# Retention of the later chunks in 64x64 matmuls, four abreast, with the decay in a table of masks

## The chip, the cores and the metric

The kernel runs on one core of one Trainium2 chip. The metric is the device time of one execution in microseconds. Five engines matter: TensorE (PE in the profile; PEld are its weight loads), VectorE (DVE), ScalarE (ACT), GpSimd (POOL) and the queue that issues the DMAs (SP). Each engine works through its own instructions in the order in which they were written, and waits on semaphores for the others. Matmuls write to PSUM, which has eight banks of 512 fp32 columns for each of 128 partitions.

## What is computed

Four sequences of 576 tokens with eight heads of 64 go through a causal linear attention with a decay for each head (retention), and the result through two feed-forward layers. Cut to its core:

```python
scores = q @ k.T / sqrt(64)                     # per batch and head, 576 x 576
gamma  = 1 - 2.0 ** (-5 - arange(8))            # one decay for each head
ret    = scores * where(rel >= 0, gamma ** rel, 0)   # rel = query - key
x      = (ret @ v), heads side by side          # 2304 tokens x 512
x      = relu(x @ w1_in) ** 2 @ w1_out          # 512 -> 2048 -> 512
h      = x @ w2_in
out    = (h * clip(h + 3, 0, 6) / 6) @ w2_out
```

All arrays are fp32.

## The kernel before

**Phases and blocks.** Phase 0 is retention and the first layer, phase 1 the second layer. The 2304 tokens are cut into five blocks of 512 or 384 for either phase (`BLOCKS`). A block takes 16 steps `f`, one for each 128 of the 2048 hidden features. In a step the main loop (from line 443) writes, in this order: `h_part` of the step after (12 matmuls of line 288 into `h`, then ACT's and DVE's work that makes `g` of `h`: lines 298 to 308), one piece of retention, and `a_part` of this step (12 matmuls of lines 329 or 331, which add to the accumulators `acc`). The operands of these matmuls are split into a high and a low part of type fp32r, so there are three products of each. So on PE a step is 12 matmuls `h`, the piece of retention, and 12 matmuls `acc`, and `acc` of a step waits for the `g` that ACT and DVE make.

**Weights.** In block 0 the weights of the first layer come in and are unpacked, step by step: ACT scales them (lines 110, 111), DVE joins the halves (126, 127) and casts every second tile (136), ACT casts the others (138), and POOL makes the low part (140, `w`). This is written between the pieces above, so all of it stands in the same queues.

**Retention.** The tokens are also cut into 18 chunks of 128. Chunks 0 to 3 are done before the first block; the chunks of block b+1 are done during block b, one chunk in four steps: slot 0 `prep_chunk` (POOL multiplies q by gamma^(t+1)/8, line 187, and v by gamma^-(t+1), line 189), slot 1 `scores`, slot 2 `values`, slot 3 `states` and the loads of the chunk two ahead. A chunk's pieces:

- `scores` (line 204): for each of eight heads k^T q, 64 rows of weights by 128 columns, fp32. Two heads lie in the two halves of the rows, in two banks `sc0` and `sc1`. DVE multiplies each bank by a mask of ones and zeros into `p` (line 208).
- `values` (line 221): for each head v^T p, 128 rows by 64 columns, two heads in the two halves of the columns, into one bank `o`; then, where a sequence doesn't begin with the chunk, four full matmuls of the running state with q (line 231). ACT and DVE split `o` into the two parts of `x` (239, 242).
- `states` (line 254): for each head k^T v, into `st`; DVE adds the old state (268) or only scales (266), and multiplies by gamma^128 (269; POOL does that from chunk 4 on).

A sequence has 4.5 chunks: chunks 0 and 9 begin one (`fresh`), 4 and 13 hold the end of one and the beginning of the next (`straddle`), 8 and 17 end one (`ends`, no state is made).

**PSUM.** Four banks hold `acc` (and the scores of chunks 0 to 3), two hold `h` (tag "h"), two hold everything else of retention (tag "at": `sc`, `o`, `st` in turns). The last of the first four chunks makes `o` in two halves (`parts=2`).

An fp32 matmul is two passes in the built program, each a weight load and a matmul of its own, and so two records in the trace; an fp32r matmul is one.

Of the kernel before, what the change touches and what calls it, by code (L numbers as in the profile page):

```python
# [32 lines left out]

VD0 = 0
GC0 = VD0 + H
MK0 = GC0 + NPAIR
QD0 = MK0 + 2 * P
NCONST = QD0 + NPAIR * P


def constants():

    gamma = 1.0 - 2.0 ** (-5.0 - np.arange(H, dtype=np.float64))
    t = np.arange(P, dtype=np.float64)
    c = np.zeros((P, NCONST), np.float64)
    for p in range(NPAIR):  # L50
        for e in range(2):
            g = gamma[2 * p + e]
            c[64 * e : 64 * e + 64, QD0 + p * P : QD0 + (p + 1) * P] = g ** (t + 1) / np.sqrt(D)
            c[64 * e : 64 * e + 64, GC0 + p] = g**P
    c[:, VD0 : VD0 + H] = gamma[None, :] ** -(t[:, None] + 1)
    causal = t[:, None] <= t[None, :]
    half = (t[:, None] < 64) == (t[None, :] < 64)
    c[:, MK0 : MK0 + P] = causal
    c[:, MK0 + P : MK0 + 2 * P] = causal & half
    return c.astype(np.float32)  # L60
# [3 lines left out]
def retention_moe_kernel(ctx: ExitStack, tc, qk, kv, w1, w2, cst, out):  # L64
# [82 lines left out]
    gc = con[:, GC0 : GC0 + NPAIR]  # L147
    state = [apool.tile([P, NPAIR, P], F32, tag=f"s{i}", name=f"state{i}") for i in range(2)]
# [6 lines left out]
    def load_chunk(c):  # L155
# [10 lines left out]
        if c == 0:  # L166
            nc.sync.dma_start(con[:, QD0:], cst[:, QD0:])
# [17 lines left out]
    def prep_chunk(c, eng):  # L185
# [5 lines left out]
    probs = {}  # L191

    def scores(c, pool=None, tag="at"):
        _, straddle, _ = where(c)
        m0 = MK0 + (P if straddle else 0)
        mask = con[:, m0 : m0 + P].unsqueeze(1).to_broadcast([P, NPAIR, P])
        q, kt, _, _ = ch[c]
        sc = [
            (pool or ps_at).tile([P, NPAIR, P], F32, tag=tag, name=f"sc{e}_{c}") for e in range(2)
        ]  # L200
        for p in range(NPAIR):
            for e in range(2):
                r = slice(64 * e, 64 * e + 64)
                nc.tensor.matmul(sc[e][:, p, :], kt[r, p, :], q[r, p, :], start=True, stop=True)  # L204
        for e in range(2):
            pool, tag = (wpool, f"w{NF - 4}_{e}") if c < n0 and c % 2 else (apool, f"p{e}")
            t = pool.tile([P, NPAIR, P], F32, tag=tag, name=f"p{e}_{c}")
            nc.vector.tensor_tensor(t, sc[e], mask, ALU.mult)  # L208
            probs[c, e] = t

    def values(c, xt, off, parts=1, then=None):
        q, _, _, v = ch[c]
        fresh, straddle, _ = where(c)
        np_ = NPAIR // parts
        for i in range(parts):
            ps = slice(i * np_, (i + 1) * np_)
            o = ps_at.tile([P, np_, P], F32, tag="at", name=f"o_{c}_{i}")
            for p in range(i * np_, (i + 1) * np_):
                for e in range(2):
                    h = 2 * p + e  # L220
                    nc.tensor.matmul(  # L221
                        o[64 * e : 64 * e + 64, p % np_, :],
                        v[:, h * D : (h + 1) * D],
                        probs[c, e][:, p, :],
                        start=p % np_ == 0,
                        stop=fresh and p % np_ == np_ - 1,
                    )
            if not fresh:
                n = 64 if straddle else P
                for p in range(i * np_, (i + 1) * np_):  # L230
                    nc.tensor.matmul(  # L231
                        o[:, p % np_, 0:n],
                        state[c % 2][:, p, :],
                        q[:, p, 0:n],
                        start=False,
                        stop=p % np_ == np_ - 1,
                    )
            hi = xt[:, 0, ps, off : off + P]
            nc.scalar.activation(hi, o, AF.Copy)
            if then is not None:  # L240
                then()
            nc.vector.tensor_tensor(xt[:, 1, ps, off : off + P], o, hi.bitcast(F32), ALU.subtract)  # L242

    def states(c):
        _, _, k, v = ch[c]
        fresh, straddle, ends = where(c)
        if ends:
            return
        k0 = 64 if straddle else 0
        st = ps_at.tile([P, NPAIR, 64], F32, tag="at", name=f"st_{c}")  # L250
        for p in range(NPAIR):
            for e in range(2):
# [3 lines left out]
                    k[k0:P, h * D : (h + 1) * D],  # L256
                    v[k0:P, h * D : (h + 1) * D],
# [3 lines left out]
        for e in range(2):  # L261
# [3 lines left out]
            if fresh or straddle:  # L265
                nc.vector.tensor_tensor(s, st[r], g, ALU.mult)
            else:
                nc.vector.tensor_tensor(s, st[r], s0, ALU.add)  # L268
                (nc.vector if c < n0 else nc.gpsimd).tensor_tensor(s, s, g, ALU.mult)  # L269
# [41 lines left out]
    def a_part(ph, blk, f):  # L311
# [4 lines left out]
        if f == 0:  # L316
            accs[ph, blk] = [
                ps_acc.tile([P, 512], F32, tag="acc", name=f"acc_{ph}_{blk}_{d}")
                for d in range(n_acc)
            ]  # L320
# [208 lines left out]
```

## Time and profile before

| | us |
|---|---|
| median of 3 runs | 886.58 (886.45 to 886.61) |
| the profiled execution | 886.73 |
| its span (first to last instruction) | 885.0 |
| PE busy in the span | 871.4 |
| DVE busy | 457.9 |
| ACT busy | 226.9 |
| POOL busy | 96.8 |
| clock granted to TensorE, mean | 0.999 |

The span is cut into engines' busy times, idle times and what ended these. Matmuls are pipelined, so two that follow each other overlap in the rows: what a matmul costs is read from the distance between starts, not from its duration. A row of the timeline has start, duration, engine, line, operation, output and inputs, shape and count, and in brackets the idle time of the engine just before with what ended it. Retention lies in the stretch from 5 to 396 us; block 0 ends on PE at 131 us, and the first layer's last block has no retention beside it.

### The profile page before, as it was taken

How to read it: one execution, taken by the hardware profiler on the slowest of the kernel's cores; microseconds unless marked ns; L12 is line 12 of the kernel's file. 1: busy time of each engine (PE TensorE's matmuls, PEld its weight loads, DVE VectorE, ACT ScalarE, POOL GpSimd, SP SyncE). 2: the span in 40 equal slices, each digit the busy share in tenths (PEclk: the TensorE clock that was granted, in tenths of full speed). 3: DMA queues.
4: the chain of work that ended last, by engine and by line, in shares of the span. 5: the costliest groups of instructions: out<-in, count | busy, mean ns of one | idle time of the engine just before them, and what ended most of it. 6: DMA issues, size and time to landing. Idle time of an engine off the chain costs nothing.

```text
span 885.0 us, 11676 instructions
## 1 busy us (share of the span) xinstructions
PE 871.4 (98%) x4752; PEld 748.3 (85%) x4752; DVE 457.9 (52%) x796; ACT 226.9 (26%) x392; POOL 96.8 (11%) x89
## 2 busy tenths in 40 slices
PE   8899999999999999999999999999999999999998
PEld 7677789999888899998888898888888888888997
DVE  6888874534434344334779776334343433343332
ACT  2556551111111111113556551111111111111111
POOL 3445550301012001110000000000000000000000
PEclk9999999999999999999999999999999999999999
DMA  9844501212110111105566300200020001000000
GB/s 335 349 156 147 198 25 72 73 48 69 44 44 24 48 48 49 48 1 170 192 214 209 131 13 1 71 1 13 1 83 1 13 13 63 0 10 35 14 1 36
DMA packets 26261, 67.73 MB, mean 77 GB/s; under 512 B 2912, under 2 KB 5088, under 8 KB 26208
## 3 DMA queue, kind: packets, MB, share of 16 engines
q1 hardware_dynamic: 26208, 67.00, 21.6%
q8 instruction: 37, 0.61, 0.3%
q14 instruction: 16, 0.13, 0.0%
HBM read 57.55 MB, written 9.44 MB: 76 GB/s over the span
## 4 chain that ended last, share of the span: by engine, by line
PE 90%; DVE 5%; issue 3%; DMA 1%; ACT 1%; SPq 0%; POOL 0%; DVEq 0%; POOLq 0%
PE h L288 41%; PE acc L331 22%; PE acc L329 20%; PE o L221 2%; PE o L231 2%; PE sc L204 1%; DVE wt L127 1%; DVE wt L126 1%; PE st L254 1%; DVE r L299 1%; ACT g L305 1%; DMA raw<-w_dram 1%; DVE p L208 1%; DMA q<-qk_dram 1%; DVE state L269 0%
## 5 line engine op out<-in xcount | busy, mean ns | idle before, releaser
L288 PE MATMUL h<-x,w 128*128 128x512 f32 (+2 forms) x1932 | 421.6, 367 | 0.0
L288 PEld LDWEIGHTS h<-x,w 128*128 128x128 f32 x1932 | 352.1, 188 | 47.6 <-POOL w L140 0.2
L329 PE MATMUL acc<-g,w 128*128 128x512 f32 (+1 forms) x960 | 215.2, 372 | 0.3 <-ACT g L305 0.3
L331 PE MATMUL acc<-w,g 128*128 128x512 f32 x864 | 210.1, 391 | 0.0
L329 PEld LDWEIGHTS acc<-g,w 128*128 128x128 f32 x960 | 172.6, 188 | 25.0 <-ACT g L305 0.7
L331 PEld LDWEIGHTS acc<-w,g 128*128 128x128 f32 x864 | 161.6, 188 | 32.6 <-DVE g L308 0.2
L302 DVE SCALAR_TENSOR_TENSOR r<-r,h 128x512 f32<-128x512 f32 (+1 forms) x80 | 50.7, 634 | 204.8 <-ACT r L301 204.6
L299 DVE TENSOR_TENSOR r<-r,h 128x512 f32<-128x512 f32 (+1 forms) x80 | 50.6, 632 | 159.9 <-ACT r L298 159.8
L301 ACT ACTIVATE r<-h,con 128x512 f32<-128x512 f32 (+1 forms) x80 | 51.7, 646 | 310.3 <-PE h L288 304.7
L308 DVE TENSOR_TENSOR g<-r,g 128x512 fp32r<-128x512 f32 (+1 forms) x160 | 105.9, 662 | 16.2 <-ACT g L305 11.2
L298 ACT ACTIVATE r<-h 128x512 f32<-128x512 f32 (+1 forms) x80 | 44.1, 552 | 245.6 <-PE h L288 238.4
L307 DVE CAST g<-r 128x512 fp32r<-128x512 f32 (+1 forms) x144 | 58.6, 407 | 14.3
L140 POOL TENSOR_TENSOR w<-wt,w 128x512 fp32r<-128x512 f32 x32 | 44.1, 1377 | 55.7 <-ACT w L138 36.1
L127 DVE CUSTOM_DVE_ANT_0 wt<-raw,wt 128x1024 uint16<-128x1024 uint16 x64 | 47.5, 742 | 3.9
L110 ACT ACTIVATE raw<-raw 128x512 f32<-128x512 f32 x64 | 42.5, 664 | 1.0 <-DMA raw<-w_dram 1.0
L111 ACT ACTIVATE raw<-raw 128x512 int32<-128x512 uint32 x64 | 42.5, 664 | 0.0
L138 ACT ACTIVATE w<-wt 128x512 fp32r<-128x512 f32 x48 | 29.6, 626 | 18.9 <-DVE wt L127 18.9
L269 POOL TENSOR_TENSOR state<-state,con 64x256 f32<-64x256 f32 x18 | 11.1, 617 | 206.9 <-DVE state L268 206.2
L126 DVE TENSOR_SCALAR wt<-raw 128x512 int32<-128x512 int32 x64 | 30.1, 470 | 0.5 <-issue 0.3
L221 PE MATMUL o<-p,kv 128*64 128x128 f32 x288 | 21.1, 279 | 4.7 <-DVE x L242 2.3
L187 POOL TENSOR_TENSOR q<-q,con 128x512 f32<-128x512 f32 x17 | 22.8, 1341 | 22.4 <-DMA q<-qk_dram 21.8
L221 PEld LDWEIGHTS o<-p,kv 128*64 128x64 f32 x288 | 15.9, 136 | 10.2 <-DVE p L208 3.9
(32 smaller groups left out, 288.0 us busy)
## 6 DMA issues: line engine op xcount, KB each, us to landing
raw<-w_dram SPq DMA_DIRECT2D x64, 512.0 KB, 5.6
q<-qk_dram SPq DMA_DIRECT2D x36, 256.0 KB, 3.1
kv<-kv_dram SPq DMA_DIRECT2D x14, 512.0 KB, 3.4
out_dram<-ev SPq DMA_DIRECT2D x18, 256.0 KB, 2.0
x<-ev SPq DMA_DIRECT2D x12, 256.0 KB, 2.3
x1r<-x SPq DMA_DIRECT2D x12, 256.0 KB, 4.3
kv<-kv_dram SPq DMA_DIRECT2D x8, 256.0 KB, 6.2
x<-ev SPq DMA_DIRECT2D x8, 192.0 KB, 1.9
```

Source lines behind the costliest of these rows:

```text
L127: nc.vector.tensor_tensor(ti, ti, low, ALU.add)
L140: eng.tensor_tensor(w[:, 1, :], t, w[:, 0, :].bitcast(F32), ALU.subtract)
L221: nc.tensor.matmul(o[64 * e : 64 * e + 64, p % np_, :], v[:, h * D : (h + 1) * D], probs[c, e][:, p, :], start=p % np_ == 0, stop=fresh an ...
L288: nc.tensor.matmul(hp[:, ts], w[:, wi, c * P : (c + 1) * P], x[:, xi, c, ts], start=k == 0, stop=k == 3 * NC - 1,)
L298: nc.scalar.activation(r, hp[:, :nb], AF.Relu)
L299: nc.vector.tensor_tensor(r, r, hp[:, :nb], ALU.mult)
L301: nc.scalar.activation(r, hp[:, :nb], AF.Relu, bias=con3)
L302: nc.vector.scalar_tensor_tensor(r, r, 6.0, hp[:, :nb], ALU.min, ALU.mult)
L307: nc.vector.tensor_copy(g[:, 0, :nb], r)
L308: nc.vector.tensor_tensor(g[:, 1, :nb], r, g[:, 0, :nb].bitcast(F32), ALU.subtract)
L329: nc.tensor.matmul(acc[d][:, :nb], wt[:, sl], gt, start=first, stop=stop)
L331: nc.tensor.matmul(acc[d], gt[:, sl], wt, start=first, stop=stop)
```

## The change

- **Chunks 4 to 17, shape.** Every product of scores, values and states is cut into 64x64 tiles of weights. Two halves of the keys of two heads stand on the four quarters of the PE array: the row half says which group of heads (0 to 3 or 4 to 7), the column half which head of a pair. The scores of keys 0 to 63 meet 128 queries, those of keys 64 to 127 only the 64 that come after; where a chunk straddles two sequences both halves meet 64.
- **PSUM.** Retention has one tile of two banks, one bank for each row half. `sc` takes 384 columns of each, the states the other 128; later the same tile is `o`. The accumulators are two tiles of two banks.
- **Decay.** The mask is now a table with gamma^rel/8 in it (`con` from `DK0` on, 776 columns, loaded by a DMA of its own behind the first weights), so q and k of the scores are used as they come. DVE multiplies 768 columns in one operation (two of 256 where the chunk straddles).
- **States** come directly behind the scores in the same slot, of k scaled by gamma^(127-t) (`scale_k`, POOL, slot 0); POOL multiplies the old state by gamma^128 beforehand (`age_state`, slot 0) and DVE adds. q for the state product is scaled behind the scores (`scale_q`, POOL, slot 1). Slot 3 only loads.
- **Block 0** begins its three chunks two steps later (f = 2 in place of 0).
- **Loads** of k and v come in two DMAs of 64 partitions, so that a row half holds its group of heads.
- **Chunks 0 to 3** keep their products; the scores of a chunk are one tile of two banks with one multiplication of 1024 columns, `o` lies in the banks of `h`, and the fourth chunk isn't cut in halves any more.

Cut to its core:

```diff
-    ps_acc = ctx.enter_context(tc.tile_pool(name="ps_acc", bufs=4, space=bass.MemoryType.PSUM))
+    ps_acc = ctx.enter_context(tc.tile_pool(name="ps_acc", bufs=2, space=bass.MemoryType.PSUM))
     ps_h = ctx.enter_context(tc.tile_pool(name="ps_h", bufs=2, space=bass.MemoryType.PSUM))
-    ps_at = ctx.enter_context(tc.tile_pool(name="ps_at", bufs=2, space=bass.MemoryType.PSUM))
+    ps_at = ctx.enter_context(tc.tile_pool(name="ps_at", bufs=1, space=bass.MemoryType.PSUM))
...
-            nc.sync.dma_start(kv_t, kv[c])
+            for g in range(2):
+                nc.sync.dma_start(
+                    kv_t[64 * g : 64 * g + 64].rearrange("t x (r e) -> t x r e", r=2),
+                    kv[c, :, :, 4 * D * g : 4 * D * (g + 1)].rearrange("(r t) x e -> t x r e", r=2),
+                )
...
+    def first_scores(c):
+        sc = ps_acc.tile([P, 2, NPAIR, P], F32, tag="acc", name=f"sc_{c}")
...
+        nc.vector.tensor_tensor(
+            t.rearrange("p e n t -> p (e n) t"), sc.rearrange("p e n t -> p (e n) t"), mask, ALU.mult
+        )
...
+    def first_values(c, xt, then=None):
+        o = ps_h.tile([P, NPAIR, P], F32, tag="h", name=f"o_{c}")
...
+    def scale_q(c):
+        if where(c)[0]:
+            return
+        nc.gpsimd.tensor_tensor(q, q, qd3, ALU.mult)
+
+    def scale_k(c):
+        if where(c)[2]:
+            return
+        nc.gpsimd.tensor_tensor(k3, k3, kd.unsqueeze(2).to_broadcast([P, H, D]), ALU.mult)
...
+    def scores(c):
+        at = ps_at.tile([P, 2, 512], F32, tag="at", name=f"sc_{c}")
+        sc = at[:, :, : 2 * MKW].rearrange("p e (j t) -> p e j t", j=2)
+        for j in range(2):
+            for i, keys in enumerate(halves(2)):
+                ts = span(c, i)
+                for g, rg in enumerate(halves(2)):
+                    for e, re in enumerate(halves(2)):
+                        nc.tensor.matmul(
+                            sc[rg, e, j, P * i : P * i + ts.stop - ts.start],
+                            kt[re, 2 * g + j, keys],
+                            q[re, 2 * g + j, ts], start=True, stop=True)
+        if not ends:
+            st = at[:, :, 2 * MKW :].rearrange("p g (j d) -> p g j d", j=2)
+            for j in range(2):
+                for i in range(first, 2):
+                    for g, rg in enumerate(halves(2)):
+                        for e, re in enumerate(halves(2)):
+                            h = 4 * i + 2 * j + e
+                            nc.tensor.matmul(st[re, g, j, :],
+                                k[rg, h * D : (h + 1) * D], v[rg, h * D : (h + 1) * D],
...
+            nc.vector.tensor_tensor(
+                t.rearrange("p e j t -> p e (j t)"), at[:, :, : 2 * MKW],
+                decay.rearrange("p e j t -> p e (j t)"), ALU.mult)
+        for e, re in enumerate(halves(2)):
+            s = diagonal(c + 1, e)
+            if fresh or straddle:
+                nc.vector.tensor_copy(s, st[re])
+            else:
+                nc.vector.tensor_tensor(s, st[re], s, ALU.add)
...
+    def age_state(c):
+        for e, re in enumerate(halves(2)):
+            nc.gpsimd.tensor_tensor(diagonal(c + 1, e), diagonal(c, e), g, ALU.mult)
...
-                j, slot = f // 4, f % 4
+                j, slot = divmod(f - 2 if blk == 0 else f, 4)
...
                     if slot == 0:
-                        prep_chunk(c, nc.gpsimd)
+                        scale_k(c)
+                        age_state(c)
                     elif slot == 1:
                         scores(c)
+                        scale_q(c)
                     elif slot == 2:
                         values(c, xs[0, blk + 1], j * P)
                     else:
-                        states(c)
                         load_chunk(c + 2)
```

PE in block 1, steps 2 to 4, beside chunk 7, before. `sc0`, `sc1` are the two banks of scores, which alternate for eight rows; `h_0_1_2` is the `h` of phase 0, block 1, step 2, and `acc_0_1_0` the first of four accumulators.

```order
L288 MATMUL h_0_1_2_1379<-x_0_1_442,w_0_2_0_410 128x384 x12
L204 MATMUL sc0_7_1398<-q_7_897 128x128
L204 MATMUL sc1_7_1399<-q_7_897 128x128
...
L288 MATMUL h_0_1_4_1470<-x_0_1_442,w_0_4_0_538 128x384 x12
L254 MATMUL st_7_1489<-kv_7_898 64x64 x8
L329 MATMUL acc_0_1_0_1363<-g_0_1_3_1440,w_0_3_1_541 128x384 x2
```

The same place in the changed kernel:

```order
L427 MATMUL h_0_1_2_1420<-x_0_1_430,w_0_2_0_398 128x384 x12
L316 MATMUL sc_7_1439<-q_7_1019 64x128 x4
L316 MATMUL sc_7_1439<-q_7_1019 64x64 x4
L316 MATMUL sc_7_1439<-q_7_1019 64x128 x4
L316 MATMUL sc_7_1439<-q_7_1019 64x64 x4
L331 MATMUL sc_7_1439<-kv_7_1020 64x64 x16
...
L427 MATMUL h_0_1_4_1543<-x_0_1_430,w_0_4_0_508 128x384 x12
```

Eight matmuls of scores became 16 smaller ones, and the states, 16 matmuls in place of eight, moved up two steps into the same visit; behind `h_0_1_4` no retention stands any more.

POOL in block 0 before: `w` is a tile of weights in work (phase, step, half). `q_4` and `kv_4` belong to chunk 4, which stands among the tiles of steps 1 to 3.

```order
L140 TENSOR_TENSOR w_0_1_1_416<-wt_0_1_1_413,w_0_1_1_416 128x512
L187 TENSOR_TENSOR q_4_221<-q_4_221,con_92 128x512
L189 TENSOR_TENSOR kv_4_222<-kv_4_222,con_92 128x512
L140 TENSOR_TENSOR w_0_3_0_473<-wt_0_3_0_447,w_0_3_0_473 128x512
L140 TENSOR_TENSOR w_0_2_1_476<-wt_0_2_1_470,w_0_2_1_476 128x512
```

POOL in the changed kernel, the same stretch and a little further:

```order
L158 TENSOR_TENSOR w_0_1_1_404<-wt_0_1_1_401,w_0_1_1_404 128x512
L158 TENSOR_TENSOR w_0_3_0_457<-wt_0_3_0_433,w_0_3_0_457 128x512
L158 TENSOR_TENSOR w_0_2_1_460<-wt_0_2_1_454,w_0_2_1_460 128x512
L158 TENSOR_TENSOR w_0_4_0_508<-wt_0_4_0_486,w_0_4_0_508 128x512
L158 TENSOR_TENSOR w_0_3_1_511<-wt_0_3_1_505,w_0_3_1_511 128x512
L293 TENSOR_TENSOR kv_4_217<-kv_4_217,con_92 128x512
L158 TENSOR_TENSOR w_0_5_0_560<-wt_0_5_0_538,w_0_5_0_560 128x512
L158 TENSOR_TENSOR w_0_4_1_563<-wt_0_4_1_557,w_0_4_1_563 128x512
L287 TENSOR_TENSOR q_4_216<-q_4_216,con_92 128x512
```

Chunk 4's work moved two steps down, and k and q are a step apart.

DVE at the end of the first four chunks, before. `x_0_0` is block 0's input of the first layer, `wt` a tile of weights in work, `st_3` and `state` belong to the states of chunk 3:

```order
L242 TENSOR_TENSOR x_0_0_157<-o_2_0_315,x_0_0_157 128x4x128
L242 TENSOR_TENSOR x_0_0_157<-o_3_0_332,x_0_0_157 128x2x128
L242 TENSOR_TENSOR x_0_0_157<-o_3_1_341,x_0_0_157 128x2x128
L126 TENSOR_SCALAR wt_0_0_1_350<-raw_0_0_1_144 128x512
L127 ISA wt_0_0_1_350<-raw_0_0_1_144,wt_0_0_1_350 128x1024
L268 TENSOR_TENSOR state0_93<-st_3_363,state1_94 64x4x64
```

And in the changed kernel:

```order
L257 TENSOR_TENSOR x_0_0_158<-o_2_306,x_0_0_158 128x4x128
L257 TENSOR_TENSOR x_0_0_158<-o_3_323,x_0_0_158 128x4x128
L144 TENSOR_SCALAR wt_0_0_1_338<-raw_0_0_1_144 128x512
L145 ISA wt_0_0_1_338<-raw_0_0_1_144,wt_0_0_1_338 128x1024
L279 TENSOR_TENSOR state0_93<-st_3_351,state1_94 64x4x64
```

The two halves of chunk 3's `o` became one operation of 512 columns; nothing else moved here.

## Rows read from the trace of the kernel before

**Rows 1.** Page, part 1: busy us, share, instructions of each engine

```profile
PE 871.4 (98%) x4752; PEld 748.3 (85%) x4752; DVE 457.9 (52%) x796; ACT 226.9 (26%) x392; POOL 96.8 (11%) x89
```

**Rows 2.** Chain that ended last, shares by line, 42:104 and then 131:400 us

```profile
by line: issue 32.1%; DVE wt L126 10.8%; DMA raw<-w_dram 8.6%; DVE wt L127 8.5%; DVE r L299 7.8%; ACT g L305 7.3%; DVE p L208 6.2%; PE acc L329 4.4%; PE h L288 4.4%; PE o L221 2.5%; PE o L231 1.8%; DVE state L266 1.4%; DVE g L308 1.2%; DVE 
...
by line: PE acc L329 43.3%; PE h L288 42.0%; PE sc L204 4.5%; PE o L221 4.2%; PE o L231 4.0%; PE st L254 2.1%
```

**Rows 3.** Timeline of PE in block 1, where `h` and retention begin

```profile
186.47 2.25 PE L288 MATMUL h<-x,w 128*128 128x384 f32 x12
...
191.88 2.25 PE L288 MATMUL h<-x,w 128*128 128x384 f32 x12
...
196.86 2.24 PE L288 MATMUL h<-x,w 128*128 128x384 f32 x12
...
201.02 2.24 PE L288 MATMUL h<-x,w 128*128 128x384 f32 x12
...
206.48 2.24 PE L288 MATMUL h<-x,w 128*128 128x384 f32 x12
...
209.68 1.16 PE L231 MATMUL o<-q,state 128*128 128x128 f32 x8
210.59 2.35 PE L329 MATMUL acc<-g,w 128*128 128x384 f32 x12
212.78 2.92 PE L288 MATMUL h<-x,w 128*128 128x512 f32 x12
```

**Rows 4.** Scores: instructions at work in short windows (second pair PE, third PEld)

```profile
183.18:183.19 0.01, 0.01 (x2) 0.01 (x2) 0.00 (x0) 1.00 0.00 0
183.19:183.39 0.20, 0.20 (x2) 0.20 (x4) 0.00 (x0) 1.00 0.00 0
```

**Rows 5.** Timeline of PE: states and values of chunk 0

```profile
11.08 0.69 PE L254 MATMUL st<-kv 128*64 128x64 f32 x16
...
11.59 1.05 PE L221 MATMUL o<-p,kv 128*64 128x128 f32 x16
```

**Rows 6.** States of chunk 2, which waited: weight loads begun in growing windows (xN)

```profile
18.17:18.21 0.04, 0.02 (x1) 1.00 0.80 307
...
18.17:18.29 0.12, 0.10 (x4) 1.00 1.05 410
```

**Rows 7.** Busy time by DVE's steps in block 0 (length; then PE, PEld, DVE, ACT, POOL)

```profile
92.72:100.29 7.57, 7.50 (x44) 5.92 (x43) 6.66 (x8) 4.00 (x7) 5.49 (x4) 1.00 0.76 301
100.29:107.13 6.84, 5.99 (x40) 4.61 (x40) 5.94 (x10) 3.98 (x7) 2.81 (x2) 1.00 0.02 4
107.13:113.40 6.27, 6.27 (x42) 4.96 (x41) 5.36 (x9) 4.35 (x8) 2.71 (x2) 1.00 0.32 101
...
120.42:126.08 5.66, 5.66 (x27) 4.69 (x26) 4.76 (x8) 2.90 (x5) 2.81 (x2) 1.00 0.00 0
```

**Rows 8.** Timeline of DVE in block 0

```profile
73.98 0.69 DVE L308 TENSOR_TENSOR g<-r,g 128x512 fp32r<-128x512 f32 x1 [0.70 <-ACT g L305]
...
94.11 1.74 DVE L308 TENSOR_TENSOR g<-r,g 128x512 fp32r<-128x512 f32 x1 [0.70 <-ACT g L305]
...
102.27 1.28 DVE L208 TENSOR_TENSOR p<-sc,con 128x512 f32<-128x512 f32 x2
...
115.38 0.87 DVE L268 TENSOR_TENSOR state<-st,state 64x256 f32<-64x256 f32 x2
```

**Rows 9.** Split of `o`: ns min/median/max over both shapes

```profile
L242 DVE TENSOR_TENSOR x<-o,x x19: 415/691/695, 13.3 to 395.3; 128x512 fp32r<-128x512 f32 x17, 128x256 fp32r<-128x256 f32 x2
```

**Rows 10.** Timeline, all engines, end of the first four chunks and step 0

```profile
26.92 0.43 DVE L242 TENSOR_TENSOR x<-o,x 128x256 fp32r<-128x256 f32 x1 [1.48 <-ACT x L239]
...
37.82 0.68 DVE L299 TENSOR_TENSOR r<-r,h 128x512 f32<-128x512 f32 x1
...
41.07 1.16 PE L204 MATMUL sc<-q 64*128 64x128 f32 x16 [2.00 <-POOL q L187]
```

**Rows 11.** Timeline of PE where block 0 ends

```profile
128.26 2.88 PE L329 MATMUL acc<-g,w 128*128 128x512 f32 x12
130.98 2.27 PE L288 MATMUL h<-x,w 128*128 128x384 f32 x12
```

More of the change, by code (lines that the diff above doesn't have):

```diff
@@ L203, in scores @@
                 r = slice(64 * e, 64 * e + 64)
[L204 to L211, printed above, removed]
-        q, _, _, v = ch[c]
[L213 to L242, printed above, removed]
@@ L245, in states, with first_states @@
+    def first_states(c):
         _, _, k, v = ch[c]
[L246 to L249, printed above, removed]
         st = ps_at.tile([P, NPAIR, 64], F32, tag="at", name=f"st_{c}")
@@ new lines, in diagonal @@
+    def diagonal(c, e):
+        re = slice(64 * e, 64 * e + 64)
+        return state[c % 2][re, :, re].rearrange("p (g j) d -> p g j d", g=2)
+    def age_state(c):
+        fresh, straddle, ends = where(c)
+        if fresh or straddle or ends:
+            return
+        for e, re in enumerate(halves(2)):
+            g = gc[re].rearrange("p (g j) -> p g j", g=2).unsqueeze(3).to_broadcast([64, 2, 2, 64])
+            nc.gpsimd.tensor_tensor(diagonal(c + 1, e), diagonal(c, e), g, ALU.mult)
@@ new lines, in values @@
+    def values(c, xt, off):
+        q, v = ch[c][0], ch[c][3]
+        fresh, straddle, _ = where(c)
+        at = ps_at.tile([P, 2, 512], F32, tag="at", name=f"o_{c}")[:, :, : 2 * P]
+        o = at.rearrange("p g (j t) -> p g j t", j=2)
+        for j in range(2):
+            for i in range(2):
+                ts = span(c, i)
+                for g, rg in enumerate(halves(2)):
+                    for e, re in enumerate(halves(2)):
+                        h = 4 * i + 2 * j + e
+                        nc.tensor.matmul(
+                            o[re, g, j, ts],
+                            v[rg, h * D : (h + 1) * D],
+                            probs[c][rg, e, j, P * i : P * i + ts.stop - ts.start],
+                            start=j == 0 and i == 0,
+                            stop=fresh and j == 1 and i == 1,
+                        )
+        if not fresh:
+            n = 64 if straddle else P
+            for p in range(NPAIR):
+                nc.tensor.matmul(
+                    o[:, p // 2, p % 2, 0:n],
+                    state[c % 2][:, p, :],
+                    q[:, p, 0:n],
+                    start=False,
+                    stop=p % 2 == 1,
+                )
+        x4 = xt[:, :, :, off : off + P].rearrange("p x (g j) t -> p x g j t", g=2)
+        hi = x4[:, 0]
+        nc.scalar.activation(hi, o, AF.Copy)
+        nc.vector.tensor_tensor(x4[:, 1], o, hi.bitcast(F32), ALU.subtract)
@@ L316, in a_part @@
         if f == 0:
-            accs[ph, blk] = [
-                ps_acc.tile([P, 512], F32, tag="acc", name=f"acc_{ph}_{blk}_{d}")
-                for d in range(n_acc)
+            two = [
+                ps_acc.tile([P, 2, 512], F32, tag="acc", name=f"acc_{ph}_{blk}_{d}")
+                for d in range(2)
             ]
+            accs[ph, blk] = [two[d // 2][:, d % 2, :] for d in range(n_acc)]
         acc = accs[ph, blk]
@@ L411, in retention_moe_kernel @@
         if c + 1 < n0:
-            scores(c + 1, ps_acc, "acc")
-            states(c)
+            first_scores(c + 1)
+            first_states(c)
         if c == 1:
```

135 lines of the change are left out of this document (103 added, 32 removed).

## The prediction

> **What bounds the kernel now.** I read the page's busy times first: PE is busy for 871 of 885 us, DVE for 458, so most of the time is PE's [rows 1]. Then the chain of waits in two stretches, since a share over the whole span hides stages [rows 2]. From 131 us on, through blocks 1 to 3, the chain is PE alone: `acc`, `h`, and about 15% of retention on lines 204, 221, 231 and 254. There a microsecond less on PE is a microsecond less of time. From 42 to 104 us, in block 0, the chain names DVE (weights on lines 126 and 127, `r`, `p`) and ACT's `g`, with PE's sequencer waiting between ("issue"). So in block 0 DVE's steps set the pace, and PE's own savings there are worth nothing. The third view is PE's timeline in block 1 [rows 3], where the distance between starts gives the price of a piece of retention; the fourth is the length of DVE's steps in block 0 [rows 7].
>
> The profiled execution took 886.73 us, its span 885.0, the median of the runs is 886.58. My sums are differences, so I put them on the median.
>
> **Blocks 1 to 3: prices before.** A step without retention takes 201.02 - 196.86 = 4.16 us; with a fresh chunk's `o` 191.88 - 186.47 = 5.41, with scores 206.48 - 201.02 = 5.46; with `o` and the state product 212.78 - 206.48 = 6.30 [rows 3]. So scores cost 1.30, fresh `o` 1.25, `o` with state 2.14, and the states, in the step from 191.88 to 196.86, 4.98 - 4.16 = 0.82.
>
> What is in a visit: the state product's eight records take 210.59 - 209.68 = 0.91, or 0.114 for a pass of 128 columns [rows 3]. The states of chunk 0, 16 records two abreast, take 11.59 - 11.08 = 0.51, or 0.064 for a pair of passes of 64 columns [rows 5]. Scores before are 16 records two abreast: eight periods of 0.114 are 0.91, which leaves 0.39 for turning PE from `h` to retention and back. States: 0.82 - 8 x 0.064 = 0.31. Fresh `o`: 1.25 - 0.91 = 0.34. I take 0.35 for a visit.
>
> **Blocks 1 to 3: after.** Four tiles abreast share one period. Scores are 16 matmuls, 32 records, four groups of 128 columns and four of 64: 4 x 0.114 + 4 x 0.064 = 0.71. States are 16 matmuls in eight groups of 64: 0.51. Both in one visit with one turn: 0.71 + 0.51 + 0.35 = 1.57, against 1.30 + 0.82 = 2.12 before: -0.55. `o` is 0.71 in place of 0.91: -0.20. A normal or fresh chunk gives -0.75, and eight of those fall in blocks 1 to 3 (7, 9 to 12, 14 to 16): -6.0. The straddle, 13, meets 64 columns only: 0.51 + 0.26 + 0.35 = 1.12 (-1.00) and `o` 0.51 (-0.40): -1.4. The ends, 8 and 17, have no states: scores 1.06 (-0.24) and `o` -0.20, twice: -0.9. Together -8.3.
>
> What must keep up beside it: `p` of 768 columns on DVE takes 0.69 + 0.28 = 0.97, by 691 ns for 512 columns and 415 for 256 [rows 9], and the state's two additions 0.87 [rows 8]. Both lie behind scores, under 4.16 of `acc` and `h` before `o` needs them; without that cover they would cost 1.84 a chunk. POOL's three scalings of a chunk lie under whole steps, as POOL is busy for 97 us in all [rows 1]. The accumulators in two tiles of two banks, the single tile of retention, and loads in two DMAs I cost at nothing: a tile is used again only a step or more later, and SP's queue now holds loads that no longer stand behind `states`.
>
> **Start, chunks 0 to 3.** DVE leads. Of its work goes: the wait of 1.48 for ACT at 26.92 [rows 10], which came from cutting chunk 3's `o` in two; one operation in place of two of 256 columns, 2 x 0.415 - 0.69 = 0.14 [rows 9]; and one mask operation in place of two for the last chunk, taken as 0.14 too. `r` of step 1 moves from 37.82 to 36.1 [rows 10]. The table of 776 columns is a new DMA behind the first weights; it is used some 20 us later than these, so I cost it at nothing. If it does delay a weight, it eats this gain.
>
> **Block 0.** A DVE step without retention is 5.66; with `p` 6.84, with `x` 6.27 (so 0.61), with POOL's two scalings beside it 7.57, or +1.9 [rows 7]. The reason stands in DVE's `g`: 0.69 alone, 1.74 while POOL works, so 1.06 for one of POOL's operations [rows 8]. The second case also shows that POOL's work isn't free for DVE. After: chunk 4, the straddle: k 1.06, q 1.06, `p` in two operations and two copies 0.83 + 0.87, `x` 0.61: 4.4. Chunk 5: k and the old state 1.9, q 1.06, `p` and additions 0.97 + 0.87, `x` 0.61: 5.4. Chunk 6: k and state 1.9 before its scores. So the last chunk's `r` comes at 36.1 + 11 x 5.66 + 4.4 + 5.4 + 1.9 = 110.1, and from `r` to the end of `p` it is 0.68 + 0.70 + 0.69 + 1.06 + 0.97 = 4.1: 114.2. Behind it PE is the chain: `o` 1.94 and five half steps of 2.72 [rows 11], 15.5, so block 1's first `h` begins at 129.7. Before it was 130.98 [rows 11]: -1.2. The two steps that chunks 4 to 6 begin later are in this. The pause of 2.00 at 41.07, where scores waited for POOL's q [rows 10], is gone, but DVE's steps take its place. Bounds: q scaled a step later may run beside operations that don't mind it, 3 x 1.06 less: -4.4; or each of the 11 steps is 0.2 longer, as steps of one kind differ: +1.0.
>
> **Sum:** 886.6 - 1.2 - 8.3 = 877.1.
>
> **Rivals.** First, a **floor on issue**. I need a record (a load with its matmul) every 0.015 to 0.028 us; the fastest long run shown is 0.51 / 16 = 0.032 [rows 5], which is also what the array allows there, so the row doesn't say which limits. For a floor speaks that after a wait four weight loads needed about 0.1 us to begin [rows 6]; against it, that two matmuls begin within 0.015 us [rows 4]. At 0.032, a group of four takes 0.128 whatever its columns: scores and states 64 x 0.032 + 0.35 = 2.40 (+0.28), `o` 1.02 (+0.11), so +3.1 for eight chunks, -0.1 for the straddle, +0.4 for the ends: 886.6 - 1.2 + 3.4 = 888.8, a little slower. Halfway to the need, at 0.025, a group of 64 columns takes 0.100: scores and states 0.46 + 0.40 + 0.80 + 0.35 = 2.01 (-0.11), `o` 0.86 (-0.05), -1.3 for eight chunks, -0.7 for the straddle, -0.3 for the ends: 883.1.
>
> The Trainium skill ("TensorE: Matmul & The Clock Gate", Part 1, "Wait — 56ns, not 53.3ns?") says that starts of matmuls never come closer than about 25 ns. By that the halfway case would hold; the trace's two starts within 15 ns disagree for a pair [rows 4], and no row here shows a long run of four.
>
> Second, the **slower side: order**. An fp32 product is two records behind each other. If the records begin strictly as written, the second pass of one tile stands between it and the next tile, and only two of the four tiles overlap. Then scores take 8 x 0.114 + 8 x 0.064 = 1.42, states 16 x 0.064 = 1.02, with 0.35 2.79 (+0.67), `o` 1.42 (+0.51): +9.4 for eight chunks, -0.1 for the straddle, +2.0 for the ends. 886.6 - 1.2 + 11.3 = 896.7. It decides as soon as the gain of four abreast falls under the doubled number of records. Against it: scores of two heads begin within 0.015 us although the first one's second pass is written between them, and nothing more begins until 0.2 us later [rows 4]. This is also how the change would not do what it says.
>
> The same page of the Trainium skill (Part 2, "Step-by-step") has matmuls stay in program order, with only weight loads pulled ahead. By that this rival would hold; the two starts speak against it [rows 4].
>
> Third, **block 0 paced otherwise**: POOL's q doesn't slow DVE, -3.2 more: 873.9.
>
> **How the numbers follow.** The forecast 0.50, block 0 better 0.07, the partial floor 0.18, a floor or a delay that eats just the gain (885 to 888) 0.08, the full floor 0.10, order 0.07. A measurement here tells about 0.2%, 1.8 us, from no change. Faster: 0.50 + 0.07 + 0.18 = 0.75; same 0.08; slower 0.17. The range from 872 to 885 holds the first three and a part of the fourth, about 0.8.
>
> **What would show it.** In the profile after, four matmuls of scores should begin within about 0.03 us, with groups 0.114 and 0.064 apart; a visit of scores and states should lengthen a step by 1.57, `o` by 1.95 with the state product. Starts evenly spaced at 0.025 or more mean the floor; starts two by two mean order. `r` of step 1 should stand at 36.1, block 1's first `h` at 129.7, and DVE's `g` should read 1.7 where q is scaled. The prediction falls if PE waits for `p` or for the state before `o` in blocks 1 to 3, or if a step without retention is no longer 4.16.

## The result and the profile after

The changed kernel takes 875.84 us (median, 874.99 to 876.31), the kernel before 886.60 in the same comparison: a ratio of 0.9875 with an interval from 0.9858 to 0.9892. It is faster by 10.8 us. The forecast was 877.1 in a range from 872 to 885. The profiled execution is the fastest of the runs, 874.99 with a span of 873.2, so rows of the two traces differ by 11.8 us in all.

The page's busy times, to be read beside [rows 1]: PE lost 12 us of work although it has 608 matmuls more, and still fills 98% of the span.

```profile
PE 859.1 (98%) x5360; PEld 742.2 (85%) x5360; DVE 460.7 (53%) x779; ACT 227.0 (26%) x391; POOL 96.2 (11%) x86
```

PE's timeline after (start, duration, engine, line, operation, tiles, shape, count; in brackets the idle time before and what ended it), to be read beside [rows 3] and [rows 11]: block 1's first `h`, the step with `o` of chunk 7 from `h` to `h`, a step without retention, a chunk's scores with states, the two steps of the straddling chunk 13, and a step at the border of the layers.

```profile
126.98 2.27 PE L427 MATMUL h<-x,w 128*128 128x384 f32 x12
...
141.70 2.25 PE L427 MATMUL h<-x,w 128*128 128x384 f32 x12
...
147.81 2.24 PE L427 MATMUL h<-x,w 128*128 128x384 f32 x12
...
190.77 2.24 PE L427 MATMUL h<-x,w 128*128 128x384 f32 x12
...
194.93 2.25 PE L427 MATMUL h<-x,w 128*128 128x384 f32 x12
197.10 0.90 PE L316 MATMUL sc<-q 64*64 64x128 f32 x32
197.82 0.65 PE L331 MATMUL sc<-kv 64*64 64x64 f32 x32
...
200.59 2.25 PE L427 MATMUL h<-x,w 128*128 128x384 f32 x12
...
267.48 2.88 PE L427 MATMUL h<-x,w 128*128 128x512 f32 x12
...
274.01 2.88 PE L427 MATMUL h<-x,w 128*128 128x512 f32 x12
...
281.21 2.88 PE L427 MATMUL h<-x,w 128*128 128x512 f32 x12
...
475.00 2.27 PE L427 MATMUL h<-x,w 128*128 128x384 f32 x12
477.59 2.35 PE L471 MATMUL acc<-w,g 128*128 128x512 f32 x9 [0.32 <-DVE ev L492]
479.78 2.27 PE L427 MATMUL h<-x,w 128*128 128x384 f32 x12
```

A step without retention is still 194.93 - 190.77 = 4.16. Scores and states together lengthen it to 200.59 - 194.93 = 5.66, by 1.50. `o` with the state product makes 147.81 - 141.70 = 6.11, by 1.95. Block 1 begins 4.0 us earlier than in [rows 11], and at the border `acc` waits for DVE's eviction `ev`, which it did not do before: that step takes 479.78 - 475.00 = 4.78.

How four abreast look, in the scores of chunk 7 and then its states (window, its length, busy time and number of matmuls at work in it, granted clock, DMA share, GB/s), to be read beside [rows 4]:

```profile
138.20:138.24 0.04, 0.03 (x4) 1.00 0.00 0
138.24:138.36 0.12, 0.12 (x4) 1.00 0.00 0
138.36:138.40 0.04, 0.04 (x8) 1.00 0.00 0
...
138.92:139.37 0.45, 0.44 (x32) 1.00 0.00 0
```

Four matmuls begin within 0.04 us, none in the next 0.12, then four more. All 32 records of the states have begun within 0.45 us, one every 0.014.

### The profile page after: what moved, and what is told of

Same layout as the page of the kernel before. It is cut to its first block, busy times and chain, and to the rows that moved or that the text cites. A ratio compares the mean times of both kernels' runs of the same rounds, so it can differ in the third digit from the quotient of the medians.

```text
span 873.2 us, 12869 instructions
## 1 busy us (share of the span) xinstructions
PE 859.1 (98%) x5360; PEld 742.2 (85%) x5360; DVE 460.7 (53%) x779; ACT 227.0 (26%) x391; POOL 96.2 (11%) x86
## 4 chain that ended last, share of the span: by engine, by line
PE 90%; DMA 4%; DVE 3%; issue 2%; ACT 1%; POOL 1%; SPq 0%; DVEq 0%; POOLq 0%
PE h L427 42%; PE acc L471 23%; PE acc L469 21%; PE o L398 2%; DMA kv<-kv_dram 1%; PE o L388 1%; PE sc L316 1%; DMA q<-qk_dram 1%; DMA raw<-w_dram 1%; PE sc L331 1%; DVE wt L145 1%; POOL w L158 0%; DVE wt L144 0%; DVE r L438 0%; ACT g L444 0%
## 5 line engine op out<-in xcount | busy, mean ns | idle before, releaser
L469 PEld LDWEIGHTS acc<-g,w 128*128 128x128 f32 x960 | 174.4, 189 | 24.7 <-ACT g L444 1.6
L447 DVE TENSOR_TENSOR g<-r,g 128x512 fp32r<-128x512 f32 (+1 forms) x160 | 108.2, 677 | 16.2 <-ACT g L444 11.2
L446 DVE CAST g<-r 128x512 fp32r<-128x512 f32 (+1 forms) x144 | 65.1, 452 | 14.7 <-DVE r L438 0.5
L287 POOL TENSOR_TENSOR q<-q,con 128x512 f32<-128x512 f32 x13 | 18.2, 1402 | 174.8 <-issue 114.8
L156 ACT ACTIVATE w<-wt 128x512 fp32r<-128x512 f32 x48 | 29.6, 627 | 15.6 <-DVE wt L145 15.5
L158 DVE TENSOR_TENSOR w<-wt,w 128x512 fp32r<-128x512 f32 x32 | 21.3, 685 | 0.0
L444 ACT ACTIVATE g<-r 128x512 fp32r<-128x512 f32 x16 | 10.1, 632 | 30.6 <-DVE r L438 30.6
L154 DVE CAST w<-wt 128x512 fp32r<-128x512 f32 x16 | 16.6, 1036 | 0.5
```

The source lines that it names most:

```text
L158: eng.tensor_tensor(w[:, 1, :], t, w[:, 0, :].bitcast(F32), ALU.subtract)
L446: nc.vector.tensor_copy(g[:, 0, :nb], r)
L447: nc.vector.tensor_tensor(g[:, 1, :nb], r, g[:, 0, :nb].bitcast(F32), ALU.subtract)
L469: nc.tensor.matmul(acc[d][:, :nb], wt[:, sl], gt, start=first, stop=stop)
```

## The experiments

Each stands beside the changed kernel at 875.84, where nothing else is said.

**Two abreast.** The same matmuls, written row half by row half (scores shown; `o` and the states alike).

```diff
-        for j in range(2):
-            for i, keys in enumerate(halves(2)):
-                ts = span(c, i)
-                for g, rg in enumerate(halves(2)):
+        for g, rg in enumerate(halves(2)):
+            for j in range(2):
+                for i, keys in enumerate(halves(2)):
+                    ts = span(c, i)
                     for e, re in enumerate(halves(2)):
```

> The changed kernel (875.84 us) with the same small matmuls written row half by row half, so that only two of the four quarters stand as neighbours in the program. Theory: what pays is that four neighbours share a period. Two abreast, by the periods read after the change (0.112 for 128 columns, 0.058 for 64), scores take 1.36 in place of 0.72, states 0.93 in place of 0.47, o 1.36 in place of 0.72: +1.75 for a normal chunk, +1.15 for the straddle, +1.28 for each end, +17.7 in blocks 1 to 3, and some more in block 0: 893 to 897 us. Rival 1: PE finds tiles that are free far ahead in its queue, so the order doesn't matter: 875 to 877 us. Rival 2: the gain came from fewer columns (64 queries for the later keys), not from four abreast: the two-abreast form would still beat the kernel before, under 886 us.

Measured: 886.37 us, against the kernel before 1.0001 (0.9991 to 1.0010). PE's timeline of chunk 7 in this kernel:

```profile
136.71 2.25 PE L427 MATMUL h<-x,w 128*128 128x384 f32 x12
138.89 1.06 PE L316 MATMUL sc<-q 64*64 64x128 f32 x26
139.68 0.27 PE L331 MATMUL sc<-kv 64*64 64x64 f32 x1
139.78 0.28 PE L316 MATMUL sc<-q 64*64 64x128 f32 x2
...
143.04 2.25 PE L427 MATMUL h<-x,w 128*128 128x384 f32 x12
...
149.53 0.33 PE L427 MATMUL h<-x,w 128*128 128x384 f32 x1
```

The step with scores and states is 143.04 - 136.71 = 6.33 in place of 5.66 (+0.67), the one with `o` 149.53 - 143.04 = 6.49 in place of 6.11 (+0.38): +1.05 a chunk where +1.75 was expected, so the time is under the 893 to 897 expected. The rows say why it is less: states (line 331) begin at 139.68, while scores (line 316), which are all written ahead of them, still begin at 139.78. By these starts PE lets a matmul whose quarter is free pass others that wait for theirs, so a part of the two row halves overlaps even when written apart. But it doesn't reach far enough. The order of writing is worth 10.5 us; the first rival (order doesn't matter) and the second (fewer columns would do) both fall. That this is just the whole gain is chance. From the first `h` of block 1 to that of block 4 the traces show 256.6 us in the changed kernel, 265.6 before and 267.3 here: two abreast, the new form is 1.7 us worse than the old one in these blocks. Block 1 begins 3.3 us earlier than before (127.66), which pays for that and for the 1.1 that the accumulators lose (below).

**States in a visit of their own**, in slot 3, with a tile of their own and the same 64x64 matmuls.

```diff
                     else:
+                        states(c)
                         load_chunk(c + 2)
```

> The changed kernel with the states in a visit of their own in slot 3, as before the change, but still in 64x64 matmuls four abreast. Theory: a visit costs PE a turn beside its matmuls; the step with scores and states is 1.50 us longer than one without, of which 0.72 and 0.47 are the matmuls, so a turn is about 0.31. Nine chunks of blocks 1 to 3 have states: +2.8, 878.6 us; a step with states alone should be 0.78 longer than one without. Rival: turns cost next to nothing behind a short visit, and the shape alone makes the gain: within 0.5 us of 875.8.

Measured: 879.96 us, +4.1. PE's timeline:

```profile
137.94 2.25 PE L431 MATMUL h<-x,w 128*128 128x384 f32 x12
...
143.13 2.25 PE L431 MATMUL h<-x,w 128*128 128x384 f32 x12
...
149.25 2.24 PE L431 MATMUL h<-x,w 128*128 128x384 f32 x12
151.42 0.69 PE L353 MATMUL st<-kv 64*64 64x64 f32 x32
...
154.24 2.24 PE L431 MATMUL h<-x,w 128*128 128x384 f32 x12
```

Scores alone take 143.13 - 137.94 - 4.16 = 1.03, states alone 154.24 - 149.25 - 4.16 = 0.83. Together they are 1.86, in one visit 1.50: a turn is 0.36 (0.31 was expected), nine times 3.2 us. Block 1 begins 1.9 us later in this trace as well (128.89), and the two traces differ by 5.4 us where the medians differ by 4.1. Of the 1.9, 1.4 arise in one early step (DVE's `r` at 36.07 and 43.14, in the changed kernel at 35.79 and 41.50), where PE's `h` waited 2.20 us for a tile of weights (0.83 in the changed kernel); whether other executions have that wait isn't shown. The rows also tell what four abreast do for the states: 0.83 alone, and 0.82 before the change. Twice as many matmuls, twice as many abreast, is the same. The states gained by moving in with the scores and by nothing else.

**Accumulators in four tiles of one bank.**

```diff
-            two = [
-                ps_acc.tile([P, 2, 512], F32, tag="acc", name=f"acc_{ph}_{blk}_{d}")
-                for d in range(2)
-            ]
-            accs[ph, blk] = [two[d // 2][:, d % 2, :] for d in range(n_acc)]
+            accs[ph, blk] = [
+                ps_acc.tile([P, 512], F32, tag="acc", name=f"acc_{ph}_{blk}_{d}")
+                for d in range(n_acc)
+            ]
...
+    first_stack.close()
+    ps_acc = ctx.enter_context(tc.tile_pool(name="ps_acc", bufs=4, space=bass.MemoryType.PSUM))
```

> The changed kernel with the accumulators in four tiles of one bank again (the scores of the first four chunks have a pool of their own, closed before the first accumulator). Theory: with tiles of two banks an eviction waits for both banks, which cost 0.5 us where the second layer begins (acc waited for an eviction at 477.3) and 0.6 at the end of the kernel (the first eviction begins 3.7 us after the last matmuls begin, before it was 3.0): 874.7 us. Rival: the waits move to another engine and the time stays at 875.8.

Measured: 874.51 us, -1.3, with runs from 873.63 to 875.99 that overlap those of the changed kernel; the traces decide. ACT's last evictions in the changed kernel (span 873.2), then the first of them with four tiles (span 871.9):

```profile
868.12 1.29 ACT L494 ACTIVATE ev<-acc 128x512 f32<-128x512 f32 x2 [2.93 <-PE acc L471]
```

```profile
866.69 0.60 ACT L495 ACTIVATE ev<-acc 128x512 f32<-128x512 f32 x1 [2.23 <-PE acc L472]
```

In tiles of two banks the first eviction waits until both banks are complete, 3.71 us after the last group of `acc` began at 864.41; with one bank each it begins beside the second bank's matmuls, 3.01 us after that group began at 863.68. The first output's DMA follows the first eviction, and the end comes 0.6 us earlier. At the border of the layers the step that was 4.78 with the wait at 477.59 is 4.18, as before the change (4.19); the step behind it gives back 0.1 of that:

```profile
474.76 2.27 PE L429 MATMUL h<-x,w 128*128 128x384 f32 x12
...
478.94 2.27 PE L429 MATMUL h<-x,w 128*128 128x384 f32 x12
```

**Block 0's chunks from step 0 on.**

```diff
-                j, slot = divmod(f - 2 if blk == 0 else f, 4)
+                j, slot = divmod(f, 4)
```

> The changed kernel with the three chunks of block 0 begun at step 0, not two steps later. Theory: DVE sets the pace of block 0 and has the same work either way, so block 1's first h begins at the same time: 875.8 within 0.7 us. Rival: in the first steps POOL is behind with the weights, scores and states wait for its scaled k as scores waited 2.0 us for its q at 41.07 in the kernel before, and DVE stands still meanwhile: 877.5 to 878.5 us. Third possibility: with the chunks done earlier PE isn't the chain at the end of block 0 any more (it was from 108.7 us on) and up to 1 us is gained.

Measured: 874.83 us, -1.0, but block 1 begins only 0.2 us earlier in its trace, and the spans of the two traces differ by 0.1. With four accumulator tiles too:

> The changed kernel with four accumulator tiles (874.51 us, 873.63 to 875.99) and block 0's chunks begun at step 0 as well. Of the offset alone the median said -1.0 us, but the runs of both kernels overlap and block 1's first h began 0.15 us apart in the traces. Theory: the offset is worth nothing, DVE has the same work: 874.5 within 0.7 us. Rival: the median was right, and the earlier chunks save about 1 us: 873.5 or less.

Measured: 873.55 us (873.30 to 873.91; against the kernel before 0.9855, 0.9838 to 0.9871), again 1.0 under its neighbour, with block 1's first `h` at 126.38 (126.76 with the offset; the spans differ by 0.4). The rival came nearer than the theory, which allowed 873.8 at the least. So the offset brings nothing here and probably costs up to 1 us; the ranges of the runs overlap, and where that microsecond lies the traces don't show. Of the kernels that leave nothing out this is the fastest, 13 us under the one before.

**Only `o` of the first four chunks in h's banks**, in the kernel before.

```diff
-        values(c, xs[0, 0], c * P, 2 if c == 3 else 1, then)
+        values(c, xs[0, 0], c * P, ps_h, "h", then)
```

> The kernel before (886.6 us) with one part of the change: o of the first four chunks in the banks of h, the fourth chunk in one piece. The masks, and everything from chunk 4 on, as before. Theory: DVE's pause of 1.48 us at 26.92 and 0.14 of a second operation go, r of step 1 comes at about 36.1 in place of 37.82, and since DVE sets the pace to the end of block 0 the whole comes through: 884.9 us. Rival: DVE's lead is eaten later in block 0, where it waits for weights or PE: 886.6 us, r of step 1 early and block 1's first h at 131.0 as before.

Measured: 885.05 us, 0.9983 (0.9974 to 0.9991) of the kernel before. In its trace `r` of step 1 stands at 35.84 and block 1 begins here:

```profile
129.00 2.27 PE L288 MATMUL h<-x,w 128*128 128x384 f32 x12
```

That is 2.0 us before the 130.98 of [rows 11]: what DVE gained at the start came through the whole block. It also makes the early part half of the 4.0 us that block 0 gained in all.

**No scaling of k, no scaling of q in block 0.** Two kernels, each without one of POOL's parts for chunks 4 to 6.

```diff
                     if slot == 0:
-                        scale_k(c)
-                        age_state(c)
+                        if blk:
+                            scale_k(c)
+                            age_state(c)
```

```diff
                         scores(c)
-                        scale_q(c)
+                        if blk:
+                            scale_q(c)
```

> The changed kernel (875.84 us) without the scaling of k and of the old state of chunks 4 to 6 (left out altogether, so that these chunks' states are wrong). Theory: these POOL operations lengthen DVE's steps by 0.6, 1.7 and 1.7 us; without them block 1's first h begins up to 3.9 us earlier, less what PE then sets: 872 to 873.5 us. Rival: PE sets the pace of block 0 already, and nothing is gained: 875.8.

> The changed kernel (875.84 us) without the scaling of q of chunks 4 to 6 (left out, so that their state products are wrong). Theory: q is scaled while DVE works on p and the state's additions, which read PSUM, and costs DVE nothing: 875.8 within 0.7 us. Rival, as the prediction's sum had it: each q costs DVE 1.06 us, so 3.2 us less: 872.6.

Measured: 871.30 us without k and the old state, a little under the 872 to 873.5 expected, and 875.61 without q. So the first costs 4.5 us (4.1 by the traces, where block 1 begins at 122.86), and the second nothing. The changed kernel's DVE shows both in chunk 5's steps (k and state under POOL from 74.92 on, q from 82.25 on; POOL's rows behind it):

```profile
73.50 0.68 DVE L438 TENSOR_TENSOR r<-r,h 128x512 f32<-128x512 f32 x1
74.88 0.69 DVE L447 TENSOR_TENSOR g<-r,g 128x512 fp32r<-128x512 f32 x1 [0.70 <-ACT g L444]
75.49 1.27 DVE L144 TENSOR_SCALAR wt<-raw 128x512 int32<-128x512 int32 x1
76.79 0.99 DVE L145 CUSTOM_DVE_ANT_0 wt<-raw,wt 128x1024 uint16<-128x1024 uint16 x1
77.70 0.84 DVE L144 TENSOR_SCALAR wt<-raw 128x512 int32<-128x512 int32 x1
78.67 1.79 DVE L145 CUSTOM_DVE_ANT_0 wt<-raw,wt 128x1024 uint16<-128x1024 uint16 x1
...
80.84 0.68 DVE L438 TENSOR_TENSOR r<-r,h 128x512 f32<-128x512 f32 x1
82.22 0.69 DVE L447 TENSOR_TENSOR g<-r,g 128x512 fp32r<-128x512 f32 x1 [0.70 <-ACT g L444]
82.83 0.95 DVE L348 TENSOR_TENSOR p<-sc,con 128x768 f32<-128x768 f32 x1
83.70 0.86 DVE L361 TENSOR_TENSOR state<-sc,state 64x256 f32<-64x256 f32 x2
84.60 0.43 DVE L144 TENSOR_SCALAR wt<-raw 128x512 int32<-128x512 int32 x1
85.06 0.69 DVE L145 CUSTOM_DVE_ANT_0 wt<-raw,wt 128x1024 uint16<-128x1024 uint16 x1
```

```profile
74.92 1.56 POOL L293 TENSOR_TENSOR kv<-kv,con 128x512 f32<-128x512 f32 x1
76.43 1.82 POOL L375 TENSOR_TENSOR state<-state,con 64x256 f32<-64x256 f32 x2
78.64 1.28 POOL L158 TENSOR_TENSOR w<-wt,w 128x512 fp32r<-128x512 f32 x1 [0.38 <-POOL state L375]
...
82.25 1.81 POOL L287 TENSOR_TENSOR q<-q,con 128x512 f32<-128x512 f32 x1
```

Beside POOL's k and state three of the operations on the weights take 1.27, 0.99 and 0.84 us; undisturbed they take 0.43 and 0.69. The fourth, of 1.79, stands beside POOL's own part of the weights (line 158), which costs DVE about as much in a step without k: there the cast of line 154 takes 1.4 us, here 0.43. The step is 80.84 - 73.50 = 7.34 in place of 5.68. Beside q, `g` is 0.69, `p` 0.95 and the additions 0.86, and it is POOL that takes 1.81 (1.29 for the q of chunk 5 before the change). `p` and the additions read one operand from PSUM. This is what the Trainium skill ("SBUF — State Buffer", "Who interferes with whom") states: DVE and GpSimd share a pair of SBUF ports, whoever starts first holds it and the other one waits, and a DVE instruction with at most one SBUF input, outside of some fast modes, isn't concerned. The trace agrees in both halves: `g` had begun 0.03 us ahead of q and kept its 0.69.

**Who else could scale k.** Four kernels gave it to another engine. The first lets DVE do it in its pause of 0.70 us behind `r`, k in one step and the old state in the next (the place in `h_part`; the call isn't shown):

```diff
             nc.vector.tensor_tensor(r, r, hp[:, :nb], ALU.mult)
+            if meanwhile is not None:
+                meanwhile()
```

> The changed kernel (875.84 us) with k and the old state of the three chunks of block 0 scaled by DVE in place of POOL, each in the pause of 0.70 us that DVE has in every step while ACT makes the high part of g. Theory: POOL's two scalings lengthen DVE's steps by 0.6 (chunk 4) and 1.7 (chunks 5 and 6) because DVE's work on its own memory slows beside POOL's; in the pause the same work is free. DVE's chain gets 3.5 us shorter, of which PE, the next to be late, lets 2 to 3.5 through: 872.3 to 873.8 us. Rival: the slowdown was not POOL's; DVE then has 0.69 and 0.84 more to do for each chunk and g comes later by what doesn't fit into the pause: 875.8 to 877.5 us.

Measured: 876.76 us, +0.9: the theory fell. In the pause k takes 1.41 us, since POOL's part of the weights (line 158, from 73.96 to 75.26) is at work there:

```profile
74.39 1.41 DVE L293 TENSOR_TENSOR kv<-kv,con 128x512 f32<-128x512 f32 x1
...
80.59 2.58 DVE L375 TENSOR_TENSOR state<-state,con 64x256 f32<-64x256 f32 x2
```

The state makes it worse: 2.58 us in a pause of 0.70. DVE's pause was not free time but the time in which POOL works without disturbing. The same with four accumulator tiles, and then with a weight operation moved into the other pauses:

> The kernel of the run before with the accumulators in four tiles of one bank, too. Theory: the two gains lie at different places (block 0; the border of the layers and the end) and add: 1.1 to 1.3 us under the run before, 871.0 to 872.6 us. Rival: one of the two waits returns elsewhere: no lower than the run before.

> The kernel of the run before, with the pause of the other steps of block 0 filled, too: the first operation (0.43 us) of the weights that DVE unpacks behind g is done in the pause. Theory: a DVE step without retention falls from 5.67 to about 5.25, under PE's 5.44, so that PE sets the pace of block 0 as well: 1 to 2.5 us under the run before, 868.5 to 871.5 us. Rival: ACT, which scales these weights, comes late with them or with g, and the pause moves behind it: no gain, or up to 1 us lost.

Measured: 875.94 and 875.11 us. The tiles brought 0.8 of the 1.1 to 1.3 expected, and filling the pauses 0.8 where 1.0 to 2.5 was expected; neither beats the four tiles alone (874.51).

Last, ACT does the scaling, in pieces of 64 columns (k shown; the state alike):

```diff
+        for h in range(H):
+            sl = slice(h * D, (h + 1) * D)
+            nc.scalar.activation(k[:, sl], k[:, sl], AF.Copy, scale=kd[:, h : h + 1])
```

> The changed kernel with four accumulator tiles (874.5 us) and, in block 0, k and the old state of chunks 4 to 6 scaled by ACT in 64-column pieces (8 for k, 8 for the state). The run with DVE doing it in its pause lost 1.0 to 1.6 us, because POOL's part of the weights already fills that pause (k took 1.41 us there). Theory: what costs is DVE and POOL shutting each other out; ACT's work doesn't touch DVE, so DVE's steps with k fall from 7.3 to 5.7 and block 1's first h comes up to 3.5 us earlier: 871 to 872.5 us. Rival: ACT is full (4.6 us of work in a step of 5.7); eight pieces of about 0.2 us more make the weights or g late and the gain is lost: 874.5 us or more.

Measured: 879.04 us, 4.5 above the four tiles. ACT's timeline, and DVE's where it waits for ACT:

```profile
75.26 2.01 ACT L383 ACTIVATE kv<-kv,con 128x64 f32<-128x64 f32 x8
77.18 2.11 ACT L391 ACTIVATE state<-state,con 64x64 f32<-64x64 f32 x8
```

```profile
80.06 0.43 DVE L146 TENSOR_SCALAR wt<-raw 128x512 int32<-128x512 int32 x1 [2.92 <-ACT raw L130]
```

Eight pieces of k and eight of the state take 4.1 us, and the weights behind them keep DVE waiting for 2.9. The rival held. In block 0 POOL is the least bad place of the three.

## Why the prediction was right, and where its sum was off

| term | predicted, us | traces, us |
|---|---|---|
| `r` of step 1 (a part of the next row) | -1.7 (36.1) | -2.0 (35.79) |
| block 1's first `h` | -1.2 (129.7) | -4.0 (126.98) |
| blocks 1 to 3 | -8.3 | -8.9 |
| accumulators in two tiles | 0 | +1.1 |
| in all | -9.5 | -11.8 |

**Blocks 1 to 3**, where PE is the chain, came out by the steps given. Scores with states were to cost 1.57 and cost 1.50; `o` with the state 1.95 and 1.95; the straddle's scores and states 1.12 and 274.01 - 267.48 - 5.44 = 1.09; its `o` saves 7.59 - 7.20 = 0.39 (0.40 predicted). With a normal chunk at -0.81, 9 and 13 at -0.84 and -1.46 and two ends at -0.46 that is -8.9. The small excess is in the period: the 0.064 that was read from 0.51 / 8 is a period of 0.058 with a rest of the first one, and 32 records of states need 0.45 and not 0.51.

**The floor on issue** is refuted by the 32 records in 0.45 us: 0.014 each, under every floor that the rival put up. The 25 ns from one start to the next that the Trainium skill ("TensorE: Matmul & The Clock Gate", Part 1, "Wait — 56ns, not 53.3ns?") gives as the least do not hold among four tiles that lie apart in the array.

**Order.** The rival was wrong for this kernel, but its mechanism exists. By the recorded starts matmuls of free quarters do pass waiting ones, also beyond the second pass of their neighbour, as [rows 4] had suggested; the two-abreast kernel shows that this reach is limited and that neighbours in the program are what the gain hangs on. It gave up 10.5 us, not the 19.6 that the rival's strict order would have cost against the forecast.

**The start** held: the pause of 1.48 and the operations went, and the kernel with this part alone shows that the microseconds reach the end of block 0, because DVE leads there up to the last chunk's `o`. That kernel keeps the two mask operations and has `r` at 35.84 all the same, so of the terms of 0.14 the one for the mask isn't seen. The 0.3 beyond the forecast says little: in the traces of eight other kernels with the same start `r` stands between 35.51 and 36.10.

**Block 0 is the step that was mis-sized.** The sum charged 1.06 us for each of the three q's, by `g` beside POOL in [rows 8]; leaving q out changed nothing (875.61). The row was right and its use wrong: in it POOL had started ahead of `g` and both worked in SBUF, while q lies beside `p` and the additions. The last part of the prediction said that `g` should read 1.7 where q is scaled; it reads 0.69. That case stood in the text as the bound of -4.4 and as the third rival at 873.9, and the traces' -4.0 is near it. The k's were charged 1.06, 1.9 and 1.9; the steps show 0.8 (not the 0.6 that two of the expectations have), 1.7 and 1.7. The end of the path was wrong too, though it hardly shows. The sum let the last chunk's `o` follow `p`, which is done at 110.6; but `o` is written to the tile that the state's additions still read, and begins right behind these:

```profile
110.49 0.87 DVE L361 TENSOR_TENSOR state<-sc,state 64x256 f32<-64x256 f32 x2
```

```profile
111.53 0.90 PE L388 MATMUL o<-p,kv 64*64 64x128 f32 x32
```

The 0.87 that the sum left out stand against the third q's 1.06 that it had too much: from `r` at 107.63 to `o` it is 3.9, in the sum 4.1. PE's row names no wait, but only because PE came late. From 86.0 to 89.4, a little behind its wait of 1.72 us for DVE at 84.71, the granted clock was 0.50, 1.2 GHz, and PE needed 6.17 us from `o` of chunk 5 to the next `h` in place of 4.57 (a window with the columns as above):

```profile
86.80:88.00 1.20, 1.20 (x5) 0.50 0.02 7
```

The kernel without q has the 4.57, with a wait of 1.74 at the same place and a granted clock that stays at 1.00, so what made it fall isn't shown. There PE arrives in time and waits; this is its `o` of chunk 6:

```profile
111.69 0.90 PE L388 MATMUL o<-p,kv 64*64 64x128 f32 x32 [1.55 <-DVE state L361]
```

So DVE sets the pace of block 0 up to there, the half clock cost nothing in this execution, and PE takes over behind it as said: from `o` to block 1 it is 15.45 (15.5 predicted).

**The accumulators** were costed at nothing with the reason that a tile is used again only a step or more later. That holds inside a layer. At its border and at the end of the kernel nothing covers the eviction, and a tile of two banks makes it wait for the second one: 0.5 and 0.6 us, which the four tiles brought back.

So the mechanism was right, and that the total came out within 1.3 us of 877.1 is in part luck: by the traces block 0 gained 2.8 us more than forecast and blocks 1 to 3 0.6 more, and the accumulators took 1.1 of that back.

## What to carry to other kernels

Small matmuls on different quarters of the array overlap if they stand next to each other in the program; write the loop over the quarters innermost, and put short visits together, since each turn away from the large matmuls cost 0.36 us here. Before another engine is given SBUF work beside a busy DVE, look at which of DVE's operations it will lie beside: next to PSUM work it was free, next to SBUF work it cost DVE half its length (1.7 us for the 3.4 of k and state), and a pause of DVE may already be in use by POOL. The granularity of a tile is the granularity of a wait: banks that are evicted one after the other want a tile each where nothing covers the eviction.

## What the runs showed of the hardware that was not expected

PE started matmuls out of the order of the program: states at 139.68 us ahead of scores at 139.78 that are written before them. The Trainium skill ("TensorE: Matmul & The Clock Gate", Part 3, "The mechanism") calls matmuls strictly first in, first out; with tiles on other rows of the array this run disagrees, at least by the recorded starts. For PE's small matmuls, then, it is not so that an engine works through its instructions strictly in the order in which they were written.

The 64x64 form gave the states nothing by itself (0.83 against 0.82 us): with half the rows in each matmul there are twice as many of them, so that four abreast only make up for it.
